# One attention kernel, three regroupings: a pair's scores and values in one piece, a causal row split 288 + 288, and two batches' first 64 tokens projected together

## The chip, the cores and the metric

One core of a Trainium2 chip. The metric is the time of one execution in microseconds (us), the median over several runs. Three runs of the kernel before gave 592.06, 592.20 and 592.43 us.

## The reference

Three layers follow one another on 4 batches of 576 tokens with 512 features, all in float32:

```python
# 1: local attention, 8 heads of 64: heads 0-3 see the last 32 keys, heads 4-7 every 4th of the last 128
scores = scale * q @ k.T;  attn = softmax(where(mask, scores, -1e9));  x = attn @ v
# 2: channel mix
xk = mu_k * x + (1 - mu_k) * x_prev;   xr = mu_r * x + (1 - mu_r) * x_prev
y = sigmoid(xr @ w_r) * (relu(xk @ w_k) ** 2 @ w_v)
# 3: four causal attention experts of 64 features, the two best of each token are summed
for e in range(4):
    a = softmax(causal(scale * (y @ wq[e]) @ (y @ wk[e]).T))
    out += gate[e] * (a @ (y @ wv[e]) @ wo[e])
```

## The kernel before

Every large product of layers 2 and 3 is split into a high and a low part, three products with 288, 260 or 512 moving columns each. TensorE has most of the work.

**Layers 1 and 2 together.** The eight heads of a batch are four pairs. For batches 2 and 3, `attn_later` (L386) runs eight pairs, `(2,0)` to `(3,3)`, under the channel mix of batches 0 to 2. It is a generator cut into steps: `goal` (L656) lets a step through for every 1.9 portions of the mix (a portion is 12 or 24 products of L474). A pair takes six steps: `turn_qk` and the loads of the next pair's q and k; the first five blocks' scores (L280) with their softmax; the first third of the previous pair's value products (L337); the other four blocks' scores and softmax; the second third; the last third, `load_v` for the next pair, and `turn_weights`. A pair has 18 score products (64x64 tile of the array, 96 moving columns) and 20 value products (64 output columns at a time). The profile has two records for each of them, so that a piece of 10 products reads x20.

`turn_weights` (L304) transposes the weights on VectorE, writes them to DRAM (`moved`, L310) and reads them back (L313) into `rqk`, all through SyncE's one queue, which also carries the loads of q, k (L165) and v (L184 to L200). The value products wait for the read.

PSUM has eight banks of 512 floats, by tag: `sc` 2, `pt` 2, `av` 1, `mm` 3. The products of L474 go to `mm`, the scores to `sc`, each half (288 columns) of a pair's values to `av`.

**Layer 3.** A batch has five row blocks, `TB` = 64, 128, 128, 128, 128 tokens. `scores` (L834) makes the causal scores of an expert block by block, two products for each part (L850, L852); then VectorE adds the mask and takes the minimum (L856), ScalarE takes the exponential (L862). The last block has 576 keys and a bank holds 512, so it is done in two parts:

```python
parts = [(0, n)] if n <= 512 else [(64, n), (0, 64)]
```

`context` (L883) turns the weights (L897), copies them out (L902, L904) and multiplies by the values (L923, L928). `project` (L940) multiplies the context of one batch by `wo`, five row blocks of six products with 512 columns (L950), the first of them with 64 tokens. `plan` (L979) says which portions run beside which expert's context: `p0` five portions of batch 0's projection, and so on. `p3` comes last, with nothing beside it.

Which instruction stands where in an engine's queue is settled when the kernel is built, by a scheduler that takes the instructions in the order in which they are written and looks at when their operands should be ready.

Of the kernel before, what the change touches and what calls it, by code (L numbers as in the profile page):

```python
# [11 lines left out]
F32R = mybir.dt.float32r  # L12
# [9 lines left out]
def tile_dilated_attention__rwkv_channel_mix__moe_attention(  # L22
# [17 lines left out]
    nc = tc.nc  # L40
# [5 lines left out]
    CH = 288  # L46
# [214 lines left out]
    def attn_weights(ap, b, hp, qT, kT):  # L261

        dil = hp >= NP // 2
        nm = f"{b}_{hp}"
        pe = ap.tile([128, NT, WK], F32, tag="pe", name=f"pe_{nm}", bufs=2)
        st = ap.tile([128, 3, NT], F32, tag="st", name=f"st_{nm}", bufs=2)
        for t0, t1 in ((0, 5), (5, 9)):
            sc = ps("sc", f"sc_{nm}_{t0}")
# [6 lines left out]
            for t in range(t0, t1):  # L275
                k0, mask = win(dil, t)
                c0 = WK * (t - t0)
                for j in range(2):
                    h = slice(64 * j, 64 * j + 64)
                    nc.tensor.matmul(sc[h, c0 : c0 + WK], qT[h, QB * t : QB * t + QB], kT[h, k0 : k0 + WK],  # L280
                                     start=(b > 0), stop=(b > 0 or t == t1 - 1))
            if b == 0:
                nc.vector.tensor_reduce(out=st[:, 0, t0:t1], in_=sc[:, : n * WK].rearrange("p (t k) -> p t k", k=WK),
                                        axis=AX.X, op=ALU.min)
# [32 lines left out]
    def attn_values(ap, b, hp, vw, pe=None, pT=None):  # L317
# [4 lines left out]
        for i in range(3):  # L322
# [6 lines left out]
            for a in range(3):  # L329
                t = 3 * i + a  # L330
                cuts = [(0, 64)] if t != 4 else [(0, 32), (32, 64)]
                for u0, u1 in cuts:
                    p0 = QB * t + u0
                    if p0 in (0, 288):
                        av = ps("av", f"av_{nm}_{p0}")
# [50 lines left out]
    def attn_later(ap, first):  # L386

        pairs = [(b, hp) for b in range(first, B) for hp in range(NP)]
        qk, vw = {}, {}

        def load_next(n):
            if n < len(pairs):
                qk[n] = load_qk(ap, None, *pairs[n])

        load_next(0)
        behind = None
        for n, (b, hp) in enumerate(pairs):
            if hp == 0:
                new_x(b)
            if n == 0:  # L400
                vw[0] = load_v(ap, b, hp)
            qT, kT = turn_qk(ap, b, hp, qk.pop(n))
            load_next(n + 1)
            yield
            weights = attn_weights(ap, b, hp, qT, kT)
            next(weights)
            yield
            if behind:
                next(behind)
                yield  # L410
            next(weights)
            yield
            pe = run_out(weights)
            if behind:
                next(behind)
                yield
                run_out(behind)
            if n + 1 < len(pairs):
                vw[n + 1] = load_v(ap, *pairs[n + 1])
            behind = attn_values(ap, b, hp, vw.pop(n), pT=turn_weights(ap, b, hp, pe))  # L420
            yield
        yield from behind
# [257 lines left out]
    with s2:  # L680
# [153 lines left out]
        def scores(b, e):  # L834
# [7 lines left out]
            for t, (t0, tn) in enumerate(TB):  # L842
                n = t0 + tn
                tn = 128
                parts = [(0, n)] if n <= 512 else [(64, n), (0, 64)]
# [37 lines left out]
        def context(b, e):  # L883
# [47 lines left out]
            if g == 0:  # L931
                ctxs[b] = xpool.tile([128, 2, 2, S], F32R, tag=f"x{b}", name=f"ctx{b}", bufs=1)
            for src, c0, c1 in ((av0[:, 0:64], 0, 64), (av1, 64, S)):
                ch, cl = ctxs[b][:, 0, g, c0:c1], ctxs[b][:, 1, g, c0:c1]
                nc.scalar.copy(ch, src)
                nc.vector.tensor_sub(cl, src, ch.bitcast(F32))
            emitted.add(("c", b, g))
            yield

        def project(b):  # L940

            for t, (t0, tn) in enumerate(TB):
                last = b == B - 1
# [3 lines left out]
                for g in range(2):  # L947
                    ch, cl = ctxs[b][:, 0, g, :], ctxs[b][:, 1, g, :]
# [8 lines left out]
                nc.sync.dma_start(out[b, t0 : t0 + tn, :], ob[:tn])  # L957
# [13 lines left out]
        for b in range(B):  # L971
            gens[f"k{b}"] = queries_keys(b, 1)
            gens[f"p{b}"] = project(b)
            if b:
# [60 lines left out]
```

## Time and profile before

| | |
|---|---|
| median of three runs | 592.20 us |
| the profiled execution | 589.86 us |
| its span | 588.0 us |
| TensorE (PE) busy | 556.3 us, 95% |
| VectorE (DVE), ScalarE (ACT) busy | 348.2 us (59%), 337.0 us (57%) |
| chain of waits | PE 76%, DVE 8%, ACT 7% of the span |
| granted TensorE clock | 0.99 of full speed |

The profiled execution is 2.3 us under the median of the three runs; what is worked out from its rows are differences. Times of rows are microseconds from the start of the span. A product's record is longer than the time it takes in a row of products, since they overlap: the cost of one is read from start to start, or from the chain of waits.

### The profile page before, as it was taken

Reading aid. Unit: us, or ns where it says so; the run is one execution under the profiler, and the core shown is the slowest. Engines: PE = TensorE matmul, PEld = TensorE weight load, DVE = VectorE, ACT = ScalarE, POOL = GpSimd, SP = SyncE. Lnnn points to the kernel's source line nnn. Section 1 sums busy time; section 2 is a strip of 40 time slices with the busy share of each in tenths; the row PEclk is TensorE's granted clock in tenths of the full one; section 3 lists DMA queues with packets and bytes.
Section 4 is the critical chain, followed back from the end, with each engine's and each line's share of the span. In section 5 each row is a group of like instructions: output and inputs, shape, how many; then the busy total and the mean of one; then the engine's idle time right before and its main releaser. Section 6 shows DMA issues by size and latency. Waiting matters only on the chain.

```text
span 588.0 us, 12635 instructions
## 1 busy us (share of the span) xinstructions
PE 556.3 (95%) x4680; PEld 493.1 (84%) x4680; DVE 348.2 (59%) x1120; ACT 337.0 (57%) x962; POOL 79.3 (13%) x101
## 2 busy tenths in 40 slices
PE   8987688999999999999999999999998999999985
PEld 4657687888988998999989999999985988988763
DVE  3568989757755569275273334527566557556562
ACT  3789967556774356265162543226656757655762
POOL 8400000000341023030030403003003003000000
PEclk9987999999999999999999999999999999999999
DMA  9981276647455652220100230044604515415302
GB/s 173 175 306 61 71 194 144 127 79 140 111 119 118 132 131 68 57 76 37 31 1 1 52 92 2 2 99 103 163 4 119 145 58 121 97 52 139 112 7 81
DMA packets 125069, 55.89 MB, mean 95 GB/s; under 512 B 104832, under 2 KB 112080, under 8 KB 125008
## 3 DMA queue, kind: packets, MB, share of 16 engines
q1 hardware_dynamic: 124592, 54.65, 39.1%
q8 instruction: 37, 0.61, 0.4%
q0 software_dynamic: 416, 0.44, 0.4%
q14 instruction: 24, 0.20, 0.1%
HBM read 32.65 MB, written 8.26 MB: 70 GB/s over the span
## 4 chain that ended last, share of the span: by engine, by line
PE 76%; DVE 8%; ACT 7%; SPq 2%; DMA 2%; issue 2%; POOL 1%; DVEq 0%; POOLq 0%; ACTq 0%
PE v L474 17%; PE h L474 12%; PE z L474 5%; PE pv L776 5%; PE av L923 5%; PE po L950 5%; PE pt L897 4%; PE sc L280 4%; PE pk L474 4%; PE av L337 4%; PE pq L474 4%; PE sc L852 2%; PE sc L850 2%; PE pt L327 1%; DVE kl L492 1%
## 5 line engine op out<-in xcount | busy, mean ns | idle before, releaser
L474 PE MATMUL h<-xh,wk_hi 128*128 128x288 f32 x256 | 78.1, 306 | 6.7 <-ACT r L488 3.5
L474 PE MATMUL v<-kh,wv_hi 128*128 128x288 f32 x256 | 76.2, 303 | 1.0 <-DVE r L489 1.0
L474 PE MATMUL h<-xl,wk_hi 128*128 128x288 f32 x256 | 75.8, 296 | 1.4 <-DVE xl L453 1.4
L474 PE MATMUL h<-xh,wk_lo 128*128 128x288 f32 x256 | 75.7, 296 | 0.0
L474 PE MATMUL v<-kl,wv_hi 128*128 128x288 f32 x256 | 75.6, 299 | 0.0
L474 PE MATMUL v<-kh,wv_lo 128*128 128x288 f32 x256 | 75.0, 296 | 0.0
L474 PEld LDWEIGHTS h<-xh,wk_hi 128*128 128x128 f32 x256 | 47.9, 188 | 9.7 <-ACT r L488 4.4
L862 ACT ACTIVATE pe<-pe,st 128x64 f32<-128x64 f32 (+4 forms) x80 | 44.8, 560 | 16.2 <-DVE st L856 16.0
L464 POOL TENSOR_TENSOR xl<-m,xh 128x1152 fp32r<-128x1152 f32 x12 | 32.0, 2671 | 162.8 <-DMA rqk<-in_k_dram 55.7
L474 PEld LDWEIGHTS v<-kh,wv_hi 128*128 128x128 f32 x256 | 47.7, 188 | 2.8 <-DVE r L489 1.4
L293 ACT ACTIVATE pe<-pe,st 128x96 f32<-128x96 f32 x108 | 39.2, 365 | 19.0 <-DVE st L289 18.8
L474 PEld LDWEIGHTS h<-xl,wk_hi 128*128 128x128 f32 x256 | 48.1, 188 | 1.7 <-DVE xl L453 1.7
L856 DVE CUSTOM_DVE_ANT_0 pe<-sc,cmask 128x64 f32<-128x64 f32 (+4 forms) x80 | 37.0, 474 | 19.8 <-PE sc L852 18.5
L474 PEld LDWEIGHTS v<-kl,wv_hi 128*128 128x128 f32 x256 | 47.9, 188 | 0.5
L474 PEld LDWEIGHTS h<-xh,wk_lo 128*128 128x128 f32 x256 | 48.2, 188 | 0.1
L474 PEld LDWEIGHTS v<-kh,wv_lo 128*128 128x128 f32 x256 | 48.0, 188 | 0.2
L488 ACT ACTIVATE r<-h 128x288 f32<-128x288 f32 x64 | 25.6, 409 | 36.5 <-PE h L474 29.0
L492 DVE TENSOR_TENSOR kl<-r,kh 128x288 fp32r<-128x288 f32 x56 | 33.4, 602 | 14.4 <-ACT kh L490 13.6
L474 PE MATMUL z<-xh,wr_hi 128*128 128x288 f32 x128 | 39.4, 310 | 1.8 <-ACT z L482 1.8
L450 DVE SCALAR_TENSOR_TENSOR m<-x,mus,m 128x288 f32<-128x288 f32 x64 | 29.9, 511 | 18.3 <-ACT m L449 18.3
L490 ACT CAST kh<-r 128x288 fp32r<-128x288 f32 x64 | 27.3, 431 | 22.1 <-DVE r L489 21.9
L689 POOL TENSOR_TENSOR yl<-x,yh 128x576 fp32r<-128x576 f32 x16 | 20.8, 1333 | 139.9 <-DVE sm L795 46.6
(167 smaller groups left out, 1468.7 us busy)
## 6 DMA issues: line engine op xcount, KB each, us to landing
kk<-kh SPq DMA_DIRECT2D x32, 144.0 KB, 2.7
kl<-kl SPq DMA_DIRECT2D x32, 144.0 KB, 2.7
raw_in_moe_w_k_dram<-in_moe_w_k_dram SPq DMA_DIRECT2D x4, 1024.0 KB, 9.1
raw_in_moe_w_v_dram<-in_moe_w_v_dram SPq DMA_DIRECT2D x4, 1024.0 KB, 5.6
out_dram<-ob SPq DMA_DIRECT2D x16, 256.0 KB, 2.4
rqk<-in_q_dram SPq DMA_DIRECT2D x48, 72.0 KB, 2.5
rqk<-in_k_dram SPq DMA_DIRECT2D x48, 72.0 KB, 2.6
moved<-turned SPq DMA_DIRECT2D x8, 432.0 KB, 2.9
```

The source lines that it names most:

```text
L293: nc.scalar.activation(pe[:, t, :], pe[:, t, :] if b else sc[:, c0 : c0 + WK], AF.Exp, bias=st[:, 0, t : t + 1], scale=-1.0, accum_out=st[ ...
L450: nc.vector.scalar_tensor_tensor(out=m, in0=x, scalar=mus[:, 0, w, f : f + 1], in1=m, op0=ALU.mult, op1=ALU.add)
L464: nc.gpsimd.tensor_sub(lo, m, hi.bitcast(F32))
L474: nc.tensor.matmul(o, w[:, kt, wsl], x[:, kt, :], start=(n == 0), stop=(n == last))
L488: nc.scalar.activation(r, p, AF.Relu)
L490: nc.scalar.copy(kh[:, fo, :], r)
L492: half.tensor_sub(kl[:, fo, :], r, kh[:, fo, :].bitcast(F32))
L776: nc.tensor.matmul(p, x[:, kt, t0 : t0 + tn], w[:, kt, 512:772], start=(n == 0), stop=(n == 3 * KT - 1))
L856: nc.vector.tensor_tensor_reduce(out=pe[:tn, PO[t] + c0 : PO[t] + c1], in0=sc, in1=m, scale=-0.125, scalar=(BIG if i == 0 else st[:tn, 1, ...
L862: nc.scalar.activation(pb, pb, AF.Exp, bias=st[:tn, 0, t : t + 1], scale=-1.0, accum_out=st[:tn, 2, t : t + 1])
L923: ins = nc.tensor.matmul(av1[p0 : p0 + 64, q0 - 64 : 512], vh[:kn, kb, :], w[i][:kn, c0 : c0 + S - q0], start=(kb == 0), stop=(kb == NB - 1))
L950: nc.tensor.matmul(p, x[:, t0 : t0 + tn], w[:, g, :], start=(n == 0), stop=(n == 5))
```

## The change

Three parts:

1. In `attn_weights`, for batches 2 and 3, both halves' score products are issued in one step, ahead of both softmaxes. In `attn_later` the previous pair's value products are issued right behind them as a whole, with the next pair's `load_v`. A pair still has six steps: q and k; nothing; all scores and all of the previous pair's values; the first softmax; the second; `turn_weights`. The second half of the values goes to a bank of `pt`.
2. In `scores`, the last block is split into keys 288 to 576 and 0 to 288.
3. In `context` the first 64 tokens of batches 0 and 1 (2 and 3) go to the halves of one tile, `c0`, of 128 columns. `project` leaves out the first block of an even batch; for an odd batch it does both batches' at once, and stores it with two DMAs. `plan` has one portion less of `p0` and of `p2`.

```diff
+        if b > 1:
+            for t0, t1 in ((0, 5), (5, 9)):
+                products(t0, t1)
+            yield
+        for t0, t1 in ((0, 5), (5, 9)):
+            if b < 2:
+                products(t0, t1)
+            sc = scs[t0]
...
-                        av = ps("av", f"av_{nm}_{p0}")
+                        av = ps("pt" if pT is not None and p0 else "av", f"av_{nm}_{p0}")
...
             yield
+            yield
             weights = attn_weights(ap, b, hp, qT, kT)
             next(weights)
-            yield
             if behind:
-                next(behind)
-                yield
-            next(weights)
-            yield
-            pe = run_out(weights)
-            if behind:
-                next(behind)
-                yield
                 run_out(behind)
             if n + 1 < len(pairs):
                 vw[n + 1] = load_v(ap, *pairs[n + 1])
+            yield
+            next(weights)
+            yield
+            next(weights)
+            yield
+            pe = run_out(weights)
             behind = attn_values(ap, b, hp, vw.pop(n), pT=turn_weights(ap, b, hp, pe))
             yield
...
-                parts = [(0, n)] if n <= 512 else [(64, n), (0, 64)]
+                parts = [(0, n)] if n <= 512 else [(CH, n), (0, CH)]
...
             for t, (t0, tn) in enumerate(TB):
+                if t == 0:
+                    if b % 2 == 0:
+                        continue
+                    tn = 128
...
-                    ch, cl = ctxs[b][:, 0, g, :], ctxs[b][:, 1, g, :]
+                    ch, cl = (ctxs[b][:, n, g, :] if t else heads_of[b // 2][:, n, g, :] for n in range(2))
```

How this moves the instructions, at three places. In the names, `av_2_1` is the value products of pair (2,1), `sc_2_2` the scores of pair (2,2); the lines of the changed kernel lie 13 or 14 further on (L283 and L350 for L280 and L337). Rows between with the mix's products are left out.

TensorE, from the first value product of pair (2,1) to the last, before and after:

```order
L337 MATMUL av_2_1_0_2331<-rqk_1243,vw_1_1260 64x64 x6
L280 MATMUL sc_2_2_5_2371<-kT_2_2_2253,qT_2_2_2251 64x96 x8
...
L337 MATMUL av_2_1_0_2331<-rqk_1243,vw_1_1260 64x64 x2
L337 MATMUL av_2_1_0_2331<-rqk_1243,vw_1_1260 64x32 x2
...
L280 MATMUL sc_2_3_0_2532<-kT_2_3_2502,qT_2_3_2500 64x96 x2
...
L337 MATMUL av_2_1_288_2414<-rqk_1243,vw_1_1260 64x32 x2
L337 MATMUL av_2_1_288_2414<-rqk_1243,vw_1_1260 64x64 x8
```

```order
L283 MATMUL sc_2_2_5_2369<-kT_2_2_2295,qT_2_2_2293 64x96 x5
...
L283 MATMUL sc_2_2_5_2369<-kT_2_2_2295,qT_2_2_2293 64x96 x3
L350 MATMUL av_2_1_0_2378<-rqk_1243,vw_1_1260 64x64 x8
L350 MATMUL av_2_1_0_2378<-rqk_1243,vw_1_1260 64x32 x2
L350 MATMUL av_2_1_288_2390<-rqk_1243,vw_1_1260 64x32 x2
L350 MATMUL av_2_1_288_2390<-rqk_1243,vw_1_1260 64x64 x8
```

The 20 value products stood in three places and now stand together, behind the last scores of the next pair; the scores themselves are still cut by products of the mix.

SyncE's queue, the write and the read of pair (2,1)'s turned weights, before and after:

```order
L310 DMA moved_2_1_2218<-turned_2_1_2216 128x864
L165 DMA rqk_1243<-in_q_dram 32x18x32
L200 DMA vw_1_1260<-in_v_dram 64x2x64
L200 DMA vw_1_1260<-in_v_dram 32x2x64
L200 DMA vw_1_1260<-in_v_dram 96x2x64
L200 DMA vw_1_1260<-in_v_dram 80x2x64
L200 DMA vw_1_1260<-in_v_dram 16x2x64 x2
L200 DMA vw_1_1260<-in_v_dram 80x2x64
L200 DMA vw_1_1260<-in_v_dram 96x2x64
L313 DMA rqk_1243<-moved_2_1_2218 32x4x288 x3
```

```order
L323 DMA moved_2_1_2260<-turned_2_1_2258 128x864
L165 DMA rqk_1243<-in_k_dram 32x18x32 x2
L165 DMA rqk_1243<-in_q_dram 32x18x32 x2
L326 DMA rqk_1243<-moved_2_1_2260 32x4x288 x3
```

Eight loads of v stood between the write and the read; now four loads of q and k do.

TensorE, the last scores of the last expert, `sc2_3_3_4`, to the first turned weights of that expert, `pt2_3_3`, before and after:

```order
L852 MATMUL sc2_3_3_4_0_7146<-kl2_3_1_6383,qs_3_1_6379 128x512
L897 MATMUL pt2_3_2_3_7155<-ident_66,pe2_3_2_6956 128x128 x2
L897 MATMUL pt2_3_2_3_7155<-ident_66,pe2_3_2_6956 64x128
L850 MATMUL sc2_3_3_4_1_7150<-kk_3_1_6381,qs_3_1_6379 128x64
L852 MATMUL sc2_3_3_4_1_7150<-kl2_3_1_6383,qs_3_1_6379 128x64
L950 MATMUL po_3_0_7226<-woh_4500,ctx3_7061 64x512
...
L897 MATMUL pt2_3_3_0_7170<-ident_66,pe2_3_3_7091 64x128
```

```order
L866 MATMUL sc2_3_3_4_1_7133<-kl2_3_1_6374,qs_3_1_6370 128x288
L911 MATMUL pt2_3_2_2_7107<-ident_66,pe2_3_2_6949 128x128 x4
L911 MATMUL pt2_3_2_3_7138<-ident_66,pe2_3_2_6949 128x128 x2
L911 MATMUL pt2_3_2_3_7138<-ident_66,pe2_3_2_6949 64x128
L974 MATMUL po_3_0_7209<-woh_4500,c0_2_6443 128x512
...
L911 MATMUL pt2_3_3_0_7153<-ident_66,pe2_3_3_7074 64x128
```

Before, six products of the projection stand between the last scores and the turning of their weights; now these six and seven turnings of the expert before.

## Rows read from the trace of the kernel before

**Rows 1.** Windows: busy us and (x records) of PE, PEld, DVE, ACT, POOL; clock

```profile
137.00:303.00 166.00, 164.88 (x1579) 151.94 (x1580) 96.04 (x312) 89.17 (x281) 30.80 (x19) 1.00 0.37 87
384.00:546.70 162.70, 159.76 (x1159) 140.03 (x1157) 96.26 (x404) 98.39 (x268) 15.43 (x12) 1.00 0.40 100
546.70:583.00 36.30, 33.44 (x199) 24.32 (x199) 19.35 (x70) 22.14 (x57) 0.00 (x0) 1.00 0.15 52
```

**Rows 2.** Waits of PE from 137 to 310: total us, times, longest

```profile
PE v L474 <- DVE r L489: 1.0, 1, 1.0
PE av L337 <- DMA rqk<-moved: 0.9, 1, 0.9
```

**Rows 3.** Chain of waits, two pieces: start, us

```profile
318.27 12.80 PE z L474 x96
538.46 1.39 PE po L950 x6
```

**Rows 4.** Timeline of PE around pieces of small products: start, us, ..., records

```profile
201.03 0.29 PE L474 MATMUL v<-kh,wv_lo 128*128 128x288 f32 x1
201.25 1.04 PE L280 MATMUL sc<-kT,qT 64*64 64x96 f32 x20
202.22 0.40 PE L474 MATMUL v<-kh,wv_hi 128*128 128x288 f32 x1
202.46 0.29 PE L474 MATMUL v<-kl,wv_hi 128*128 128x288 f32 x1
...
183.80 0.54 PE L280 MATMUL sc<-kT,qT 64*64 64x96 f32 x6
184.27 0.40 PE L474 MATMUL h<-xh,wk_hi 128*128 128x288 f32 x1
...
197.66 0.80 PE L337 MATMUL av<-rqk,vw 96*64 96x32 f32 x20
198.40 0.41 PE L474 MATMUL v<-kl,wv_hi 128*128 128x288 f32 x1
...
194.05 0.42 PE L337 MATMUL av<-rqk,vw 96*64 96x64 f32 x8
194.41 0.40 PE L474 MATMUL v<-kh,wv_lo 128*128 128x288 f32 x1
```

**Rows 5.** Windows of L474 alone: length, PE busy (x records), PEld busy; clock

```profile
136.90:293.80 156.90, 127.64 (x865) 116.40 (x864) 1.00 0.40 92
```

**Rows 6.** Timeline of SyncE's queue around the turned weights: start, us

```profile
161.02 0.44 SPq L310 DMA_DIRECT2D moved<-turned  x1
...
162.35 4.86 SPq L200 DMA_DIRECT2D vw<-in_v_dram  x8
167.26 1.40 SPq L313 DMA_DIRECT2D rqk<-moved  x3
...
261.93 1.39 SPq L313 DMA_DIRECT2D rqk<-moved  x3
```

**Rows 7.** Chain of waits and timeline of PE where the read weights are used

```profile
168.23 3.04 DMA rqk<-moved
...
171.51 0.57 PE L337 MATMUL av<-rqk,vw 96*64 96x64 f32 x12 [0.87 <-DMA rqk<-moved]
...
266.87 0.34 PE L337 MATMUL av<-rqk,vw 96*64 96x64 f32 x4
```

**Rows 8.** Timeline of PE, last causal block: its two parts

```profile
549.20 0.40 PE L850 MATMUL sc<-kk,qs 128*128 128x512 f32 x1
549.44 0.40 PE L852 MATMUL sc<-kl,qs 128*128 128x512 f32 x1
549.67 0.39 PE L950 MATMUL po<-woh,ctx 128*128 128x512 f32 x1
...
552.46 0.19 PE L850 MATMUL sc<-kk,qs 128*128 128x64 f32 x1
552.60 0.48 PE L950 MATMUL po<-woh,ctx 128*128 128x512 f32 x1
552.92 0.40 PE L950 MATMUL po<-wol,ctx 128*128 128x512 f32 x1
```

More of the change, by code (lines that the diff above doesn't have):

```diff
@@ L266, in attn_weights, with products @@
         st = ap.tile([128, 3, NT], F32, tag="st", name=f"st_{nm}", bufs=2)
-        for t0, t1 in ((0, 5), (5, 9)):
-            sc = ps("sc", f"sc_{nm}_{t0}")
+        scs = {}
+        def products(t0, t1):
+            sc = scs[t0] = ps("sc", f"sc_{nm}_{t0}")
             n = t1 - t0
@@ L281, in attn_weights @@
                                      start=(b > 0), stop=(b > 0 or t == t1 - 1))
+        if b > 1:
[6 more added lines that the diff above has]
+            sc = scs[t0]
+            n = t1 - t0
             if b == 0:
@@ L404, in attn_later @@
             yield
+            yield
             weights = attn_weights(ap, b, hp, qT, kT)
             next(weights)
+            if behind:
+                run_out(behind)
+            if n + 1 < len(pairs):
+                vw[n + 1] = load_v(ap, *pairs[n + 1])
             yield
-            if behind:
-                next(behind)
-                yield
+            next(weights)
+            yield
             next(weights)
@@ L413, in attn_later @@
             pe = run_out(weights)
-            if behind:
-                next(behind)
-                yield
-                run_out(behind)
-            if n + 1 < len(pairs):
-                vw[n + 1] = load_v(ap, *pairs[n + 1])
             behind = attn_values(ap, b, hp, vw.pop(n), pT=turn_weights(ap, b, hp, pe))
             yield
-        yield from behind
+        yield
+        yield
+        run_out(behind)
+        yield
     def run_out(gen):
@@ L932, in context @@
                 ctxs[b] = xpool.tile([128, 2, 2, S], F32R, tag=f"x{b}", name=f"ctx{b}", bufs=1)
+                if b % 2 == 0:
+                    heads_of[b // 2] = ep.tile([128, 2, 2, 128], F32R, tag="c0", name=f"c0_{b}", bufs=2)
             for src, c0, c1 in ((av0[:, 0:64], 0, 64), (av1, 64, S)):
-                ch, cl = ctxs[b][:, 0, g, c0:c1], ctxs[b][:, 1, g, c0:c1]
+                ch, cl = (ctxs[b][:, n, g, c0:c1] if c0 else heads_of[b // 2][:, n, g, 64 * (b % 2) : 64 * (b % 2) + 64]
+                          for n in range(2))
                 nc.scalar.copy(ch, src)
@@ L938, in context @@
             yield
+        heads_of = {}
         def project(b):
             for t, (t0, tn) in enumerate(TB):
+                if t == 0:
+                    if b % 2 == 0:
+                        continue
+                    tn = 128
                 last = b == B - 1
@@ L956, in project @@
                     nc.scalar.copy(ob[:tn], p)
-                nc.sync.dma_start(out[b, t0 : t0 + tn, :], ob[:tn])
+                if t:
+                    nc.sync.dma_start(out[b, t0 : t0 + tn, :], ob[:tn])
+                else:
+                    for i in range(2):
+                        nc.sync.dma_start(out[b - 1 + i, 0:64, :], ob[64 * i : 64 * i + 64])
                 yield
```

4 rows, old and new, of the table plan are left out of this document.

## The prediction

> **What bounds the kernel now.** I read the windows first, to learn which engine sets the pace in the stages that the change touches. The reader is to see that TensorE is busy for 164.88 of 166.00 us under the channel mix and 159.76 of 162.70 us in layer 3, at the full clock (1.00, the 2.4 GHz level), while VectorE and ScalarE have 89 to 98 us of work in each [rows 1]. Only the last 36.30 us have 2.86 us in which TensorE does nothing. So up to 546.7 us a microsecond of TensorE's work is a microsecond of the span, unless a wait opens. The waits come second: from 137 to 310 us TensorE waits 0.9 us for the turned weights of one pair and 1.0 us for VectorE, and for little else [rows 2]. The timeline comes third, from start to start, because records overlap: that is where it shows what a small product costs beyond its columns. The prices of full-size products come from the chain of waits: 12.80 us / 96 = 0.133 us for 288 columns, 1.39 us / 6 = 0.23 us for 512 columns [rows 3].
>
> **Part 1: scores and values in one piece.** No product goes away; what goes is the going in and out. Around the scores at 201.25 the piece starts 0.22 us behind the last product of the mix instead of 0.13, and the second product of the mix follows the first by 0.24 instead of 0.13 [rows 4]: 0.09 + 0.11 = 0.20 us for each stretch of small products, whatever is in it. Inside, from the piece's start to the next product of the mix, 20 records of scores take 0.97 us and 6 take 0.47, so a record costs 0.50 / 14 = 0.036 and a piece of scores 0.97 - 0.71 = 0.26 more. 20 records of values take 0.74 us and 8 take 0.36 [rows 4]: 0.032 a record and 0.11 a piece.
>
> The counts come from the order of TensorE's instructions, from the first scores of batch 2 to the last values of batch 3. Before there are 24 pieces of scores and 31 of values in 50 stretches; with the change there are 22, 17 and 31. It isn't 8, because the scheduler still lets products of the mix in wherever a piece's operands aren't ready. The fixed cost falls from 24 x 0.26 + 31 x 0.11 + 50 x 0.20 = 19.7 us to 22 x 0.26 + 17 x 0.11 + 31 x 0.20 = 13.8 us: **-5.9 us**. The model can be tested on the stage as a whole. It lasts 156.90 us and has 865 products of L474 [rows 5]; without 865 x 0.133 = 115.3 us, 41.6 us are left for the small ones. The model gives 19.7 + 288 x 0.036 + 360 x 0.032 = 41.6 us, and the one wait of 0.9 stands beside that, so it holds within a microsecond. If joining saved only the entries and exits, 19 x 0.20 = 3.8 us would be left: the lower bound.
>
> Moved with it are the loads of v. Pair (2,1)'s read of its turned weights stood behind eight loads, 4.86 us of the queue [rows 6], and landed at 168.23 + 3.04 = 171.27, just ahead of the value products that had waited 0.87 us for it [rows 7]. In the new order no loads of v lie between, so this wait goes: **-0.9 us**. The loads themselves go to the third step, behind values that free their buffer, and are needed a pair later; SyncE's queue has nothing urgent behind them until the sixth step.
>
> What is late next: now all 20 value products stand behind the same read, and the second softmax comes one step later. In pair (3,2) the read lands at about 261.93 + 1.39 + 3.04 = 266.4 and its products start at 266.87, so half a microsecond is all the slack there is [rows 6, 7]. TensorE also reaches them sooner by what it saves. I take **+1.0 us** for new waits of this kind over the eight pairs; the bounds are 0 and 8 x 0.9 = 7 us, by the one such wait that there is. I stay near the lower end because at least 124 products lie between any pair's last scores and its first values in the new order, and at least 114 before.
>
> The second bank for the values comes from `pt`, which has no other use for batches 2 and 3. The last pair ends later: its last values stand 37 products further on in TensorE's order, 37 x 0.133 = 4.9 us nearer to the receptance that needs them. Before, they end at 293.80, where I cut the stage, and that product starts at 318.27 [rows 3, 5], so 19 us are left for a mix. The wait of 1.0 us for VectorE lies in this stretch [rows 2]; it may go or double. I take 0, with -1.0 and +1.0 as bounds.
>
> **Part 2: 288 + 288 keys.** A pair of 512-column products takes 549.67 - 549.20 = 0.47 us. The pair of 64 columns takes 552.60 - 552.46 = 0.14 us and delays the product behind it, which takes 552.92 - 552.60 = 0.32 instead of 0.23: 0.23 us together [rows 8]. The new four take 4 x 0.133 = 0.53 us instead of 0.70, on TensorE's path: 0.17 x 16 experts = **-2.7 us**. VectorE reads the same 576 columns in two instructions as before, and ScalarE's exponential is unchanged.
>
> The Trainium skill, "TensorE: Matmul & The Clock Gate", section "Back-to-back issue gap", speaks against this gain: it gives N / 2.4 + 2.5 ns for a product alone and a floor of about 25 ns for the smallest, by which 512 + 64 and 288 + 288 columns cost the same 0.49 us a pair of parts, and part 2 would be worth 0. The rows differ from it: 0.23 us, not 0.03, for each short pair with what it delays.
>
> **Part 3: two first blocks in one.** Two blocks of six products go: 12 x 0.23 = **-2.8 us** [rows 3]. A block with 64 tokens costs TensorE as much as one with 128, since the 512 columns move either way. Two copies on ScalarE go too, hidden. At the end of the kernel there are still five blocks; one more store is issued there, first of the six, so that it lies beside the rest.
>
> One of the two blocks was filler in the last 36.30 us, where TensorE idles for 2.86 us [rows 1]. If the chain of an expert (scores, VectorE, ScalarE, turning, copies, values) sets the pace there, taking filler away gives nothing back. Against that, the new order puts seven turnings more between the last scores and the weights that wait for them. I take 0 for these stalls, between -1.4 and +2.8 us.
>
> **The sum.** -5.9 - 0.9 + 1.0 - 2.7 - 2.8 = -11.3 us. The rows come from an execution of 589.86 us, 2.3 us under the median of the three runs; I apply the difference to the median, 592.2 - 11.3 = **580.9 us**.
>
> **The rivals.** (a) *Layer 3 gives nothing back.* Its chains through VectorE and ScalarE take the place of TensorE, and parts 2 and 3 turn into waits: 592.2 - 5.9 - 0.9 + 1.0 = 586.4 us. For it: ScalarE has 22.14 us of work in the last 36.30 and depends on VectorE and TensorE in turn. Against it: in the 162.70 us ahead TensorE idles for less than 3 us in all [rows 1]. (b) *Part 2 gives nothing.* Scores have two banks, and a block's scores can start only when VectorE has read an earlier part. If that decides when the last block can be done, or if the 0.09 us behind a short pair is paid behind a 288-column pair too and the rest is hidden, the four products end no sooner: 580.9 + 2.7 = 583.6 us. For it: the delay is read at one place. Against it: no wait of that kind in the rows. The page named above gives the same time. (c) *Slower: the values wait for their read.* The second softmax is issued a step later, and a step is 1.9 portions of at least 12 products, 1.9 x 12 x 0.133 = 3.0 us. If every pair's read came that much later, less the slack of 0.5, TensorE would stand still for 2.5 us in each of eight pairs: 592.2 - 12.3 + 20 = 599.9 us. It decides from 12.3 / 8 = 1.5 us a pair. Before, one pair waits 0.9 and no other waits visibly; and softmaxes can be moved up by the scheduler as soon as their scores are there, which is now earlier. (d) *The pieces aren't what the diff says.* The order shows 31 stretches, not 8; that is in the sum already.
>
> **How the numbers follow.** My forecast has 0.70, (a) 0.13, (b) 0.10, (c) 0.04, and 0.03 is for what I haven't seen. The range must hold (a) and (b) and the bounds: -1.0, -1.4 and -1.0 of the three uncertain terms wouldn't all come together, so I go 3.4 us down to 577.5, and up past (a) to 587.0. A difference of 0.2% (1.2 us) is about what a measurement of this kernel can tell from none. Faster by more: the forecast, (a) and (b), 0.93. Slower: (c) and part of the unseen, 0.04. Within: 0.03.
>
> **What would show it.** Right: 31 stretches with about 35 us for small products between the first scores of batch 2 and the last values of batch 3, no wait at pair (2,1) and under 1.5 us in all for reads of turned weights; the last causal block's four products at 0.133 us from start to start; 108 products of the projection instead of 120; TensorE's busy time about 10 us lower. Wrong: waits for `rqk<-moved` at several pairs of 1 us and more, or an idle time in layer 3 that grows by what TensorE's work shrank.

## The result, and the profile after

| | before | changed |
|---|---|---|
| median | 592.13 us | 583.46 us (580.81 to 586.66) |
| ratio | | 0.9862, 95% interval 0.983 to 0.9894 |
| the profiled execution, its span | 589.86 us, 588.0 us | 580.81 us, 579.1 us |
| TensorE busy | 556.3 us | 547.8 us |
| chain of waits | PE 76%, DVE 8%, ACT 7% | PE 78%, DVE 8%, ACT 6% |

The change is faster by 8.7 us between the medians; the interval of the ratio is 6.3 to 10.1 us. The forecast was 11.3 us less than before, 580.9 us, with a range of 577.5 to 587.0. Executions of one kernel differ by some microseconds. In the profiled ones, of all kernels here, TensorE's granted clock differs in the first 130 us, which no part touches (0.66 to 0.74 from 40 to 60 us, 0.83 to 1.00 from 60 to 80), and batch 2's first scores begin between 136.5 and 141.7 us. So stages are compared by their own length.

The windows of the changed kernel, the first with the products of the mix alone (L488 is L474 of before): length, busy us (x records) of PE, PEld, DVE, ACT, POOL, clock.

```profile
137.70:293.92 156.22, 127.55 (x901) 120.74 (x900) 1.00 0.40 93
377.40:540.10 162.70, 158.26 (x1162) 140.35 (x1161) 97.43 (x404) 98.57 (x270) 15.69 (x12) 1.00 0.41 103
540.10:574.10 34.00, 30.69 (x185) 21.91 (x184) 18.76 (x70) 19.90 (x54) 0.00 (x0) 1.00 0.10 36
```

From batch 2's first scores to batch 3's last values there are 156.22 - 901 x 0.133 = 36 us for the small products, where [rows 5] left 41.6 with 36 products of the mix less; the prediction said about 35. Layer 3 shows the other side: in the same 162.70 us as in [rows 1] TensorE is busy 158.26 instead of 159.76 us.

TensorE's waits from 137 to 310 us in the changed kernel: us, times, longest. The two of [rows 2] are gone, and no value product waits for its read.

```profile
PE v L488 <- DVE x L512: 0.4, 1, 0.4
```

Two marks divide the gain: batch 2's first scores, and the first receptance product of batch 3. TensorE runs the same products between them in both kernels. Before, the timeline and [rows 3] put them at 136.88 and 318.27, 181.39 us apart.

```profile
136.88 1.04 PE L280 MATMUL sc<-kT,qT 64*64 64x96 f32 x18
```

In the changed kernel (timeline, and chain of waits) they are 174.06 us apart:

```profile
137.70 1.04 PE L283 MATMUL sc<-kT,qT 64*64 64x96 f32 x18
```

```profile
311.76 12.80 PE z L488 x96
```

So the pieces gave 7.3 us. From the second mark to the end of the span it is 588.0 - 318.27 = 269.7 us before and 579.1 - 311.76 = 267.3 now: layer 3 gave 2.4 us, and 0.8 were lost ahead of the first mark. 7.3 + 2.4 - 0.8 = 8.9 us is the difference of the spans.

What became of layer 3's share is seen in TensorE's waits from 375 to 585 us, before and after:

```profile
PE pt L897 <- DVE pe L877: 2.1, 2, 1.1
PE av L923 <- DVE wt L904: 1.1, 2, 0.7
PE pt L897 <- DVE wt L904: 0.8, 1, 0.8
PE po L950 <- DVE st L856: 0.5, 1, 0.5
PE pt L897 <- ACT wt L902: 0.5, 1, 0.5
PE pk L474 <- DVE ql L755: 0.4, 1, 0.4
PE pq L474 <- ACT yh L688: 0.2, 1, 0.2
```

```profile
PE pt L911 <- DVE pe L891: 3.4, 4, 1.1
PE sc L866 <- DMA kl<-kl: 1.2, 1, 1.2
PE av L937 <- DVE st L883: 0.7, 1, 0.7
PE av L937 <- DVE wt L918: 0.7, 1, 0.7
PE sc L864 <- DVE st L870: 0.6, 2, 0.4
PE pt L911 <- ACT wt L916: 0.5, 1, 0.5
PE av L937 <- DVE st L870: 0.2, 1, 0.2
```

They are 5.6 us before and 7.3 now. The new ones are turnings (`pt`) that wait for VectorE's scaled weights, and scores that wait for the copy of the keys' low parts.

The last expert's scores in the timeline of the changed kernel, which answer [rows 8]:

```profile
542.93 0.29 PE L864 MATMUL sc<-kk,qs 128*128 128x288 f32 x1
543.06 0.29 PE L866 MATMUL sc<-kl,qs 128*128 128x288 f32 x1
543.19 0.86 PE L974 MATMUL po<-woh,ctx 128*128 128x512 f32 x3
...
544.57 0.38 PE L864 MATMUL sc<-kk,qs 128*128 128x288 f32 x1
544.79 0.29 PE L866 MATMUL sc<-kl,qs 128*128 128x288 f32 x1
544.91 0.19 PE L864 MATMUL sc<-kk,qs 128*128 128x64 f32 x1
```

The first pair takes 0.26 us, the second, behind turnings, 0.34: 0.60 together, where the prediction had 0.53, and 0.70 before.

### The profile page after: what moved, and what is told of

It is laid out like the page before. It is cut to its first block, busy times and chain, and to the rows that moved or that the text cites. A ratio compares the mean times of both kernels' runs of the same rounds, so it can differ in the third digit from the quotient of the medians.

```text
span 579.1 us, 12606 instructions
## 1 busy us (share of the span) xinstructions
PE 547.8 (95%) x4665; PEld 491.3 (85%) x4668; DVE 347.1 (60%) x1120; ACT 334.9 (58%) x960; POOL 79.9 (14%) x101
## 4 chain that ended last, share of the span: by engine, by line
PE 78%; DVE 8%; ACT 6%; SPq 2%; DMA 2%; issue 2%; POOL 1%; DVEq 0%; POOLq 0%; ACTq 0%
PE v L488 16%; PE h L488 14%; PE z L488 7%; PE pv L790 5%; PE av L937 5%; PE sc L283 4%; PE pk L488 4%; PE pt L911 4%; PE po L974 4%; PE pq L488 4%; PE av L350 4%; PE sc L864 2%; PE sc L866 2%; SPq L165 2%; PE pt L340 1%
## 5 line engine op out<-in xcount | busy, mean ns | idle before, releaser
L488 PE MATMUL h<-xh,wk_hi 128*128 128x288 f32 x256 | 78.4, 307 | 6.6 <-ACT r L502 3.7
L488 PE MATMUL h<-xl,wk_hi 128*128 128x288 f32 x256 | 76.2, 298 | 0.1
L488 PE MATMUL v<-kh,wv_hi 128*128 128x288 f32 x256 | 75.9, 301 | 0.4 <-DVE x L512 0.4
L488 PE MATMUL h<-xh,wk_lo 128*128 128x288 f32 x256 | 75.8, 296 | 0.0
L488 PE MATMUL v<-kl,wv_hi 128*128 128x288 f32 x256 | 75.7, 298 | 0.0
L488 PE MATMUL v<-kh,wv_lo 128*128 128x288 f32 x256 | 75.0, 295 | 0.0
L488 PEld LDWEIGHTS h<-xh,wk_hi 128*128 128x128 f32 x256 | 48.5, 190 | 9.4 <-ACT r L502 4.8
L870 DVE CUSTOM_DVE_ANT_0 pe<-sc,cmask 128x64 f32<-128x64 f32 (+4 forms) x80 | 33.4, 427 | 31.3 <-PE sc L866 30.4
L488 PEld LDWEIGHTS h<-xl,wk_hi 128*128 128x128 f32 x256 | 48.6, 190 | 0.5 <-DVE xl L467 0.4
L488 PEld LDWEIGHTS v<-kh,wv_hi 128*128 128x128 f32 x256 | 47.7, 188 | 1.5 <-DVE x L512 0.6
L488 PEld LDWEIGHTS h<-xh,wk_lo 128*128 128x128 f32 x256 | 48.7, 190 | 0.0
L488 PEld LDWEIGHTS v<-kl,wv_hi 128*128 128x128 f32 x256 | 48.0, 188 | 0.5
L488 PEld LDWEIGHTS v<-kh,wv_lo 128*128 128x128 f32 x256 | 48.1, 188 | 0.1
L506 DVE TENSOR_TENSOR kl<-r,kh 128x288 fp32r<-128x288 f32 x56 | 35.0, 631 | 13.6 <-ACT kh L504 13.0
L488 PE MATMUL z<-xh,wr_hi 128*128 128x288 f32 x128 | 39.1, 308 | 1.3 <-ACT z L496 1.3
L911 PE MATMUL pt<-ident,pe 128*128 128x128 f32 (+1 forms) x240 | 35.2, 274 | 3.8 <-DVE pe L891 3.4
```

The source lines that it names most:

```text
L488: nc.tensor.matmul(o, w[:, kt, wsl], x[:, kt, :], start=(n == 0), stop=(n == last))
L506: half.tensor_sub(kl[:, fo, :], r, kh[:, fo, :].bitcast(F32))
L870: nc.vector.tensor_tensor_reduce(out=pe[:tn, PO[t] + c0 : PO[t] + c1], in0=sc, in1=m, scale=-0.125, scalar=(BIG if i == 0 else st[:tn, 1, ...
L911: nc.tensor.transpose(pt[:kn, c0 : c0 + tn], pe[:tn, PO[t] + k0 : PO[t] + k0 + kn], ident[:tn, :tn])
```

## The experiments

### The whole change again, and each part alone

The first is the changed kernel once more.

> The changed kernel again. Four executions of it lay between 580.81 and 586.66 us, three to four of the kernel before within 1.7 us. Theory A: the spread comes from where it ran (another chip), so that five rounds on one chip agree within 1.5 us and the ratio to the kernel before is 0.981 (-11.3 us, the sum of my terms) or near the profiled 0.985 (-8.9 us). Theory B: something in the changed kernel waits in some executions and not in others; then the rounds spread over 4 us or more on one chip, and the kernel before does not.

Measured: 582.69 us, ratio 0.9858 (0.9829 to 0.9887). The six executions lie within 4.1 us, but those of the kernel before spread as much (589.22 to 595.53), so neither theory holds as it was put. Between the two marks lie 174.07 us (138.33 to 312.40) again. Layer 3 took 268.5 us instead of 267.3; a fall of the clock, shown further on, took 1.7 us of it.

Part 1 alone, its pieces of the diff on the kernel before, of which two are shown:

```diff
+        if b > 1:
+            for t0, t1 in ((0, 5), (5, 9)):
+                products(t0, t1)
+            yield
...
             if behind:
-                next(behind)
...
                 run_out(behind)
```

> Part 1 alone (scores and values of batches 2 and 3 in one piece). My sum: -5.9 - 0.9 + 1.0 = -5.8 us. The trace of the whole change shows the receptance of batch 3 starting 6.5 us earlier than before (311.76 against 318.27), and 0.8 us lost ahead of batch 2, so a theory by the trace says -6.5. Rival: a part of it is taken back by waits in layer 3, which begins at another phase of its queues: -4 or less.

Measured: 584.01 us, ratio 0.9876 (0.9852 to 0.99), 7.3 us less than before. The marks are 174.08 us apart (137.98 to 312.06), as in the whole change, and layer 3 takes 269.3 us, 0.4 less than before. Part 1 is worth all that the stage shows, and hardly anything beyond it.

Part 2 alone:

```diff
-                parts = [(0, n)] if n <= 512 else [(64, n), (0, 64)]
+                parts = [(0, n)] if n <= 512 else [(CH, n), (0, CH)]
```

> Part 2 alone (288 + 288 keys). My sum: -2.7 us, from 16 x 0.17. Rival a (layer 3 gives nothing back): between -0.8 and +0.5, with more waits of TensorE between 384 and 583 us than the 5.6 us of before. Rival by the gap formula (equal columns, equal time): 0, and then the four products of a split row would take as long as before, 0.70 us.

Measured: 593.73 us, ratio 1.0035 (1.001 to 1.0059), 2.1 us more than before, which is outside of all three forecasts. TensorE's work did shrink. From layer 3's first product to the last 16 wide value products it is 194.4 us both times, before and with part 2, but TensorE's busy time in it fell by 2.0 us:

```profile
382.42:576.83 194.41, 188.65 (x1338) 162.37 (x1337) 114.20 (x475) 119.03 (x321) 15.43 (x12) 1.00 0.36 92
```

```profile
386.55:580.92 194.37, 186.63 (x1338) 161.50 (x1337) 114.75 (x475) 118.70 (x321) 15.67 (x12) 1.00 0.36 92
```

The waits of layer 3 went from 5.6 to 7.5 us. What the short pairs had cost came back as waits, microsecond for microsecond. What layer 3 lost in the profiled execution lies behind that, in the timeline of the end of this kernel:

```profile
576.44 1.19 PE L897 MATMUL pt<-ident,pe 128*64 128x128 f32 x8 [1.18 <-DVE pe L877]
...
579.80 1.08 PE L923 MATMUL av<-wt,vt 64*64 64x512 f32 x4 [0.73 <-DVE wt L904]
...
580.92 4.07 PE L923 MATMUL av<-wt,vt 128*64 128x512 f32 x16
```

and in its windows (clock third from the end):

```profile
576.00:578.00 2.00, 1.19 (x8) 0.81 (x8) 1.28 (x5) 1.19 (x2) 0.00 (x0) 1.00 0.04 8
578.00:580.00 2.00, 1.19 (x9) 0.94 (x11) 0.91 (x3) 0.62 (x2) 0.00 (x0) 1.00 0.00 0
580.00:582.00 2.00, 2.00 (x12) 0.81 (x10) 0.23 (x1) 0.21 (x1) 0.00 (x0) 0.74 0.00 0
582.00:584.00 2.00, 2.00 (x10) 0.60 (x8) 0.00 (x0) 0.00 (x0) 0.00 (x0) 0.50 0.00 0
```

After 4 us in which TensorE was busy for 2.4, the clock fell from 2.4 to 1.2 GHz, and the 16 products took 4.07 us. Before, they took 2.38:

```profile
576.83 2.38 PE L923 MATMUL av<-wt,vt 128*64 128x512 f32 x16
```

The kernel before has the same 4 us, as thin, and kept its clock, so the thin stretch alone does not decide it:

```profile
571.91:573.91 2.00, 1.20 (x8) 0.81 (x8) 1.28 (x5) 1.19 (x2) 0.00 (x0) 1.00 0.03 8
573.91:575.91 2.00, 1.18 (x9) 0.94 (x11) 0.91 (x3) 0.61 (x2) 0.00 (x0) 1.00 0.00 0
```

Without these 1.7 us, layer 3 takes 269.7 us, as before; another 4.1 us of this execution were lost ahead of layer 3, where part 2 changes nothing. Over all executions of that comparison the mean granted clock is 0.9798 with part 2 and 0.9835 before; the missing share, times the span, is 12.0 and 9.7 us, and the mean span is 2.3 us longer. In which part of the span that share was lost is known for the profiled execution alone.

Part 3 alone, the shared block of 64 + 64 tokens:

```diff
+                if t == 0:
+                    if b % 2 == 0:
+                        continue
+                    tn = 128
```

> Part 3 alone (first 64 tokens of two batches in one block). My sum: -2.8 us, from 12 products of 0.23. Rival a: the block taken out of batch 2's projection was filler for the last experts, so only the one of batch 0 counts: -1.4, with TensorE idle longer than 2.9 us in the last 36 us. If parts 2 and 3 each give their full price and the whole change gave only 2.4 us in layer 3, they get in each other's way; if each gives half, the waits do.

Measured: 590.56 us, ratio 0.9982 (0.9964 to 1.0), 1.1 us less, where 2.8 were expected. By the same reckoning the share of the clock that is missing is 8.5 us here and 9.7 before, so the 1.1 us can be the clock alone. In the profiled execution layer 3 takes 269.2 us, 0.5 less. Its 12 products went, but TensorE's busy time in layer 3, before and with part 3, fell by 1.0 us only:

```profile
318.27:583.00 264.73, 258.93 (x1849) 229.91 (x1847) 142.28 (x527) 146.27 (x379) 27.34 (x20) 1.00 0.30 77
```

```profile
320.51:584.90 264.39, 257.91 (x1836) 228.60 (x1835) 143.53 (x528) 144.68 (x377) 27.31 (x20) 1.00 0.30 76
```

Added up from start to start, less the idle times, the products of the projection take 2.2 us less and the turnings 1.0 us more. Why the turnings do is not shown.

### The change without part 2

```diff
-                parts = [(0, n)] if n <= 512 else [(CH, n), (0, CH)]
+                parts = [(0, n)] if n <= 512 else [(64, n), (0, 64)]
```

> The change without its second part: pieces of layer 1 joined and the shared block of 64 + 64 tokens, while the long causal scores stay 512 + 64 keys. Alone, the pieces gave about -7.3 us, the block -1.1, the halves +2.1, and the whole change -8.3. Theory A (TensorE's saving by the halves is eaten by waits in layer 3): about -8.4 against before, level with the whole change within 1 us. Rival B (the halves really cost their 2.1 us, in the whole too): -10.5, some 2 us faster than the whole change. Rival C (the halves give their 2.0 us of TensorE time in the whole, where the block changes the tail): -6.4, 2 us slower than the whole change.

Measured: 581.67 us (581.11 to 582.8), ratio 0.9826 (0.9807 to 0.9845): 10.3 us less than before. By the medians rival B holds and C falls, but this interval (9.2 to 11.4 us) and the whole change's (6.3 to 10.1) overlap. The profiled executions speak for C's reading: layer 3 takes 268.8 us without part 2 and 267.3 in the whole change, both at the full clock, and TensorE's busy time is 257.63 and 254.59 us:

```profile
310.61:575.00 264.39, 257.63 (x1836) 228.60 (x1835) 143.87 (x528) 144.97 (x377) 27.36 (x20) 1.00 0.30 77
```

```profile
311.76:575.00 263.24, 254.59 (x1836) 227.73 (x1835) 143.69 (x528) 144.61 (x377) 27.60 (x20) 1.00 0.31 77
```

So beside the other parts 1.5 us of part 2 reached the end in that execution. Whether part 2 gains or costs over many executions is not settled; the clock, taken up below, has a part in it.

### Scores joined, values not

```diff
             weights = attn_weights(ap, b, hp, qT, kT)
             next(weights)
+            next(weights)
             yield
             if behind:
                 next(behind)
```

> Only one half of part 1 on the kernel before: the scores of a pair of batches 2 and 3 are issued in one go, while its value products and the loads of v stay where they were. By the program's order this makes 9 score pieces fewer, 2 value pieces more and 7 stretches fewer than before. Theory A (the prediction's fixed prices 0.26, 0.11 and 0.20 us): -2.3 + 0.2 - 1.4 = -3.5 us against before. Rival B (part 1's gain came from the waits that went, by way of the loads of v that now stand elsewhere, and pieces are worth little): -1 to +0.5 us, with the wait for the read of the turned weights still there.

Measured: 587.6 us, ratio 0.9921 (0.9905 to 0.9937), 4.7 us less than before; the marks are 178.41 us apart (137.48 to 315.89), 3.0 less. Theory A gave 3.5. The wait for the read was still there, 0.7 us, and the 1.0 us for VectorE too. Layer 3 takes 269.7 us, as before; where the other 1.7 us of the medians come from is not shown.

### The pieces uncut: by priority, then held in place

The change left 22 pieces of scores where 8 would do. A higher priority makes the scheduler put them together (`marks["values"]` is the last value product issued so far):

```diff
-            for t0, t1 in ((0, 5), (5, 9)):
-                products(t0, t1)
+            with tc.high_priority(), tc.issue_after(marks["values"]) if "values" in marks else ExitStack():
+                for t0, t1 in ((0, 5), (5, 9)):
+                    products(t0, t1)
...
-                run_out(behind)
+                with tc.high_priority():
+                    run_out(behind)
```

> The whole change, and on top of it a higher priority for the scores and values of batches 2 and 3, with a pair's scores queued behind the values of the pair two before: by the program's order 8 score pieces instead of 22, 8 value pieces instead of 15, 10 stretches instead of 30. Theory A (the fixed prices hold and TensorE stays the bound): 14 x 0.26 + 7 x 0.11 + 20 x 0.20 = -8.4 us against the changed kernel, some -16.7 against before (about 575 us). Rival B (the work that stood between the pieces was cover: with the stretches this long, TensorE waits for the windows, the read of the turned weights or the mix): part or all of it comes back as waits at the values or at the products of the mix, -3 to +3 against the changed kernel.

Measured: 589.02 us (587.56 to 594.35), ratio 0.9967 (0.9943 to 0.999), some 6 us more than the whole change. TensorE's waits from 130 to 330 us:

```profile
PE av L351 <- DMA rqk<-moved: 6.5, 5, 2.9
PE z L493 <- ACT xh L482: 3.2, 1, 3.2
PE sc L283 <- DVE st L312: 2.3, 1, 2.3
```

These are the waits of the prediction's rival (c), come about in another way: pairs follow each other faster than a write and a read of the turned weights can. Behind the waits the clock fell as well, to 0.69 in the window from 160 to 170 us. So the pieces were held back to where the program writes them:

```diff
+    def traced_last():
+        return next(i for i in reversed(nc.cur_bb.bb.instructions) if i.engine == mybir.EngineType.PE)
...
-            for t0, t1 in ((0, 5), (5, 9)):
-                products(t0, t1)
+            with tc.high_priority(), tc.issue_after(traced_last()):
+                for t0, t1 in ((0, 5), (5, 9)):
+                    products(t0, t1)
...
-                run_out(behind)
+                with tc.high_priority(), tc.issue_after(traced_last()):
+                    run_out(behind)
```

> The whole change, and each pair's scores and the last pair's values of batches 2 and 3 in one uncut stretch, now held back to their place in the program (issued behind the last product of the mix that was written ahead of them): 8 score pieces, 8 value pieces, 9 stretches instead of 22, 15, 30, with 82 to 158 products of the mix between two stretches. The run with a higher priority and no such hold spent 12 us in waits (read of the turned weights 6.5, the mix 3.2, a score bank 2.3). Theory A (fixed prices 0.26, 0.11, 0.20 us; those waits came from running ahead): from batch 2's first scores to batch 3's receptance 174.1 - 3.6 - 0.8 - 4.2 = 165.5 us, and the run some 8 us below the whole change. Rival B (work between the pieces was cover that long stretches need): the stretch of time stays above 171 us, with waits of 6 us and more. Rival C (the prices were an accident of how records are cut, and cutting costs little): no new waits, and 172 to 174 us.

Measured: 579.07 us (575.98 to 581.73), ratio 0.9792 (0.9761 to 0.9823), 12.3 us less than before. The marks, in the timeline and in the chain:

```profile
141.66 2.79 PE L287 MATMUL sc<-kT,qT 64*64 64x96 f32 x36
```

```profile
309.97 12.80 PE z L495 x96
```

They are 168.31 us apart, with 1.4 us of waits. The clock was low as the first mark came, and for 2.34 us behind it:

```profile
141.66:144.00 2.34, 2.34 (x31) 2.34 (x32) 0.88 (x6) 0.13 (x1) 0.00 (x0) 0.51 0.68 119
```

That is 1.1 us, and without it the stage takes 167.2; theory A said 165.5. The run is some 4 us under the whole change, where theory A said 8. The stage gave 5.8, and layer 3 took 2.0 back: it takes 269.3 us, with the clock at 0.68 from 405 to 410 us.

> The same without part 2 (scores as 512 + 64 keys). The change without part 2 was as fast as the whole or up to 1.8 us faster. Theory A: level with the run of the paced kernel within 1 us, either sign; batch 2's first scores to batch 3's receptance 165.5 us. Rival (288 + 288 costs its 2.1 us in the whole): 2 us faster than the paced kernel with halves.

Its edit is the two above together. Measured: 577.59 us (576.01 to 581.84), ratio 0.9775 (0.9745 to 0.9806), 1.5 us less than with 288 + 288 keys, intervals overlapping. The marks are 170.40 us apart (141.00 to 311.40), where 165.5 were expected, with 2.6 us of waits and a clock of 0.88 and 0.95 in the windows from 150 to 170 us, which is 1.7 us.

> The paced kernel without part 2, with the first pair's scores of batch 2 left as in the whole change (no priority, no hold), so that the order up to them is that of the whole change again: 9 score pieces, 8 value pieces, 10 stretches. The two paced kernels showed 1.6 and 1.8 us of waits just ahead of batch 2's first scores, and 1.4 us at the mix behind them, where the whole change had 0.8 and none. Theory A (holding the first pair shifted the work around it and made these waits): batch 2's first scores to batch 3's receptance 174.1 - 13 x 0.26 - 7 x 0.11 - 20 x 0.20 = 165.9 us with under 1 us of waits, 1.5 to 2.5 us faster than the paced kernel without part 2 (-15 to -16 against before). Rival B (with the pieces this long the values of batch 1's last pair and the first mix are late wherever the first scores stand): the waits stay above 2 us and the time is level with it, within 1 us.

The edit, on the kernel ahead of it:

```diff
+                if (b, hp) != (2, 0):
+                    held.enter_context(tc.high_priority())
+                    held.enter_context(tc.issue_after(traced_last()))
```

Measured: 577.15 us (575.17 to 580.45), ratio 0.9763 (0.9731 to 0.9795), level with the paced kernel without part 2: rival B. The marks:

```profile
136.85 1.04 PE L287 MATMUL sc<-kT,qT 64*64 64x96 f32 x18
```

```profile
304.60 12.80 PE z L498 x96
```

167.75 us, with 2.2 us of waits that moved to the values (1.4 for ScalarE, 0.8 for the read). By the median it is the fastest kernel of the study, 14.0 us under before and some 6 us under the change.

The prediction's prices can now be held against five kernels. Pieces and stretches are counted here from TensorE's order over all products of batches 2 and 3, by which before has 24 pieces of scores, 29 of values and 49 stretches (the prediction's counts are 2 pieces of values and 1 stretch higher on both sides). "By the prices" is 181.39 us plus the difference in fixed cost (0.26, 0.11, 0.20 us), in waits, and in what the clock took:

| kernel | pieces, stretches | waits, clock | by the prices | measured |
|---|---|---|---|---|
| before | 24, 29, 49 | 2.1 us | | 181.39 us |
| scores joined | 15, 31, 42 | 1.9 | 177.7 | 178.41 |
| the change | 22, 15, 30 | 0.4 | 173.8 | 174.06 |
| paced | 8, 8, 9 | 1.4, 1.1 | 167.3 | 168.31 |
| paced, no halves | 8, 8, 9 | 2.6, 1.7 | 169.1 | 170.40 |
| paced but first | 9, 8, 10 | 2.2 | 167.5 | 167.75 |

### Layer 3: other filler, and a clock kept up

The changed kernel's three waits for scaled weights stand between 435 and 440 us, all in one expert's step. Two projection blocks were moved ahead of them:

```diff
-                (1, 1): [("c", 6), ("s", 6)],
+                (1, 1): [("c", 6), ("p0", 2), ("s", 6)],
...
-("l2", 1), ("p0", 4), ("q2", 2)],
+("l2", 1), ("p0", 2), ("q2", 2)],
```

> The whole change, with two of batch 0's four later projection blocks given one expert earlier, so that they stand ahead of the three waits for scaled weights (2.8 us) that layer 3 of the changed kernel shows between 435 and 440 us. Theory A (TensorE stands there because nothing to fill with is in reach): those waits fall below 1 us and the run is 1.5 to 2.5 us faster than the whole change. Rival B (the chain score - exponential - scale - transpose sets the pace of layer 3, whatever fills): the waits turn up one expert earlier or later, and the time is within 0.7 us of the whole change.

Measured: 583.94 us (579.92 to 587.06), ratio 0.987 (0.9833 to 0.9908), level with the whole change: rival B. The medians alone do not decide it, since the mean clock was 0.9797 here and 0.9843 in the kernel before; but the profiled executions of both kernels kept the full clock in layer 3, and there it took 267.2 us, 0.2 less. The waits for scaled weights were still 2.2 us in three places.

What those waits can trigger is seen in the repetition of the change. Two windows of it, then the same two of the first profile of the change:

```profile
430.00:440.00 10.00, 7.22 (x51) 6.29 (x50) 8.16 (x21) 6.56 (x18) 4.84 (x4) 1.00 0.58 141
440.00:450.00 10.00, 9.79 (x63) 7.85 (x63) 5.59 (x23) 5.87 (x18) 0.57 (x1) 0.83 0.17 39
```

```profile
430.00:440.00 10.00, 7.22 (x51) 6.28 (x50) 7.93 (x21) 6.55 (x18) 5.13 (x4) 1.00 0.61 147
440.00:450.00 10.00, 9.79 (x73) 7.64 (x73) 6.49 (x26) 6.43 (x19) 0.26 (x1) 1.00 0.14 33
```

With the same order and the same idle 2.8 us, the clock falls in one execution and not in the other: 63 products instead of 73 in the next ten microseconds. Of the seven profiles of kernels with 288 + 288 keys five show such a fall in layer 3 before the last product (between 400 and 460 us, or at the end); of the seven without, none. Each of these falls took 1.7 us. With that taken off, layer 3 takes 266.8 to 267.6 us in the five profiles with the shared block and the halves (the change, its repetition, the pieces by priority, the other filler, paced; three of them with falls), and 268.7 to 268.8 us in the three with the block alone (the change without part 2, and the two paced kernels without it). So the halves save 1 to 2 us of layer 3 beside the block while the clock holds, and one fall takes that back.

So part 2 alone was run with its end kept busy by products on a tile of zeros:

```diff
+                if (b, e) == (B - 1, E - 1):
+                    last = next(x for x in reversed(nc.cur_bb.bb.instructions) if x.engine == mybir.EngineType.PE)
+                    with tc.issue_after(last):
+                        keep_warm((4, 0, 2, 0)[i])
...
+            if (b, e) == (B - 1, E - 1):
...
+                    keep_warm(3)
```

> Part 2 alone (288 + 288 keys) on the kernel before, with five products on a tile of zeros among the last expert's transposes, and, as it falls out in the order, six projection products ahead of the last value products. In the profile of part 2 alone TensorE was granted half its clock for the last expert's 16 wide value products (4.07 instead of 2.38 us). Theory A (part 2's +2.1 us is that fall of the clock after the thin stretch at the end): the 16 products take 2.4 us again and the run is level with before, -1.5 to +0.5. Rival B (the +2.1 is in layer 3's new waits, or in the ordering): still 1.5 to 2.5 us over before.

Measured: 592.65 us, ratio 1.0034 (1.0014 to 1.0055), 2.0 us more than before. The 16 products took 2.37 us again, yet theory A falls as it was put. Nine products of zeros stood there, not five:

```profile
569.82 1.03 PE L76 MATMUL idle<-still 128*128 128x512 bf16 x4
...
573.64 0.59 PE L76 MATMUL idle<-still 128*128 128x512 bf16 x2
...
575.07 0.81 PE L76 MATMUL idle<-still 128*128 128x512 bf16 x3
```

From the first of each to what follows it (570.50, 574.25, 575.53) they hold TensorE for 0.68 + 0.61 + 0.46 = 1.75 us, about where it had waited, and in the profiled execution the clock fell at the other place:

```profile
440.00:450.00 10.00, 7.20 (x40) 6.17 (x40) 7.29 (x20) 6.67 (x17) 5.37 (x4) 0.83 0.75 180
```

Layer 3 takes 271.4 us there, and 269.7 without the 1.7 us of that fall, as before, so in this execution no cost of the zeros is seen. Over all executions the mean clock was 0.9838, with 0.9844 before: it was back, and the time was not. How much of part 2's loss is the clock, and how much the order that goes with it, stays open.

## Why the prediction was right in sign and short in layer 3

**Part 1, -5.9 us, held.** Its prices were read at four places, and they give the stage of five kernels to 0.3 to 1.3 us, down to a fixed cost of 5 us where before has 19. The Trainium skill, "TensorEngine Tiling (Array Packing)", section "Key Properties", says that a change of the tiling mode drains TensorE; the 0.20 us of a stretch agree with it, though no run separates a drain from what else they hold, and the 0.26 and 0.11 us of a piece come on top.

**The wait of pair (2,1), -0.9, held**: no value product waited for a read in the changed kernel.

**New waits, +1.0, did not come.** They come, 6.5 us at five places, when the pieces run ahead (the run by priority alone), and 0.8 us at one when they are held. At the change's pace there were none: the lower bound, 0, was right.

**The wait around batch 3's mix, 0, was -0.6**: 1.0 us for VectorE became 0.4. Together -5.9 - 0.9 - 0.6 = -7.4, and 7.3 were measured, where the prediction's sum for these terms was -5.8.

**Part 2, -2.7, is the step that failed.** The price was a little too high: 0.60 us for the four products, not 0.53, since a pair behind another kind of product pays 0.09 us as well; 0.10 x 16 = 1.6 us, and with part 2 alone TensorE's busy time fell by 2.0. But the prediction took all of it for path, because TensorE was busy 98% of layer 3, and with part 2 alone the waits grew by as much. The sentence "an idle time in layer 3 that grows by what TensorE's work shrank" was named as the sign of being wrong, and it is what the profile of part 2 alone shows. In the whole change some 1.5 us came through where the clock held; falls of the clock, 1.7 us each, are no term of the prediction and took that back in three of the five profiles with both parts. The rule of the Trainium skill that was weighed ("TensorE: Matmul & The Clock Gate", "Back-to-back issue gap") gave 0 for part 2, and 0 or worse was measured for part 2 alone; but the work did shrink, so it is right about the time and not about why. By its formula a short pair would cost 0.05 to 0.06 us, not the 0.03 that the prediction holds against the 0.23.

**Part 3, -2.8, was the other term that was mis-sized**: 0.5 us of layer 3 in the profiled execution, and 1.1 us between all executions, which can be the clock. The prediction priced the 12 products as if nothing else on TensorE would change; its busy time fell by 1.0 us, not 2.8, with the turnings 1.0 us longer.

**The stalls of the end, 0, were about 0.5**: TensorE idles 34.00 - 30.69 = 3.31 us in the last window, and 2.86 us in that of [rows 1].

In sum layer 3 gave 2.4 of 5.5 us, 3.1 short, part 1 gave 1.5 more, and 0.8 were lost ahead of both. Of the rivals, (a) describes part 2 alone; in the whole change some half of part 2 and a fifth of part 3 came through while the clock held, which none of them says. That the time agrees with (b)'s 583.6 us is chance: (b) had layer 3's other term whole. (c) was seen only where it was forced.

The error is in how [rows 1] was read. A stage in which TensorE idles for 3 of 163 us need not be one in which TensorE sets the pace everywhere. Its few waits sat in the steps of a few experts; there VectorE, ScalarE and the copies of keys are just in time, and what TensorE saves in such a step can come back as a wait, as all of part 2 did when it stood alone.

## What to carry to other kernels

Count the places where small products go in and out between full ones, price a piece and a stretch from two pieces of different length, and the gain of joining them can be forecast to about a microsecond; to get it whole, pin the pieces to their place in the program, since a priority alone pulls them ahead of their operands. A saving on a busy engine can come back as waits of that engine: split the stage by steps, and look for waits in them, before summing. And try each part alone and leave each out: here one of three parts was worth nothing by itself, gave some 1.5 us beside the others, and the kernel without it was, by the medians, at least as fast.

## What the runs showed of the hardware

The same order of instructions with the same 2.8 us of idle time in ten lost TensorE's full clock in one execution and kept it in another; when it fell, some 1.7 us went with it (4.07 instead of 2.38 us for 16 products, 63 instead of 73 products in ten microseconds). The Trainium skill, "TensorE: Matmul & The Clock Gate", section "HAM oscillation — how this bites in real kernels", describes work that starts at the lower clock after waits, over and over; here a profile shows one or two falls of the clock in layer 3 or none, at places where TensorE had waited, and not in every execution: at the end of the kernel before, 4 us with 2.4 us of work kept the full clock, and with part 2 alone the same 4 us lost it. So 2 us between two kernels can be the clock alone.
